# Two fused attention batches ahead of an MoE pair: V in rows of four tokens, pooled q and k summed by VectorE, and a replanned order

## The chip, the core and the metric

The kernel runs on one core of one Trainium2 chip. The metric is device time in microseconds (us), from the first to the last instruction of the program with what lies around them; lower is better. Engines: PE is TensorE (PEld its weight loads), DVE is VectorE, ACT is ScalarE, POOL is GpSimd, SP is SyncE, which here only issues DMAs.

## What is computed

Three steps in a row, with q, k, v of 4 batches x 8 heads x 576 tokens x 64:

```python
q_d = q.reshape(B, H, Sd, 4, D).mean(axis=3)          # the same for k_d, v_d; Sd = 144
out_up = np.repeat(sm_attn(q_d, k_d, v_d), 4, axis=2) # pooled attention, repeated
mask = np.abs(pos[:, None] - pos[None, :]) < 4        # banded attention, 7 keys a query
out = out_up + softmax(mask(scale * q @ k.T)) @ v
x = out.transpose(0, 2, 1, 3).reshape(2304, 512)
h = x @ w_in;  x = (h * sigmoid(h)) @ w_out           # 512 -> 2048 -> 512
h = x @ w2_in; g = s * relu(h) ** 2 + b
return g @ w2_out
```

The two weight pairs arrive as 64-bit floats and are turned into two 32-bit halves (high and low part) on the chip, by bit operations of DVE. Each product of the two layers is three matmuls of fp32r halves.

## The kernel before

The tokens are cut into five blocks (512, 512, 512, 512, 256). `mix1(u)` does the first layer of block u: for each of 16 slices m of the hidden dimension 12 matmuls into `hp`, SiLU, and 12 into `y0` to `y3`. The second layer follows for all blocks, into `hp2` and `o`. A 512-token block is 384 matmuls of 512 columns in each layer.

The attention of a batch is done for four pairs of heads (`hq` 0 to 3). Batches 2 and 3 take the banded part on DVE (`local`). Batches 0 and 1 take it on PE. For one pair:

- `tokens` loads q and k with a token on each partition (tiles `nq`, `nk`; the last 64 tokens of all heads come once, as `zq`, `zk`), `natural` loads v with eight tokens on each of 72 partitions (`nv`), `v_load` the band's copy of v (`vw`).
- `b_turn` turns q and k on PE (`pq`, L705 and L702) and ACT or DVE copy them to `qkT` (or `qT`, `kT`).
- `down` is the pooled attention. For batch 0 its sums of four tokens are PE matmuls with a 0/1 matrix `fours` (L596, L597, tile `pd`); for batch 1 they are DVE reductions of the turned tiles (L607, L609). v is summed by two DVE additions (L583, L584). Scores `pS` (L639), softmax, turns `pT` (L662), values `pU` (L671), kept in `upT`.
- `banded`: scores `pB` (L754), mask, softmax, turns `pBT` (L787), values `pBO` (L796), and the sum with `upT` into `xf` (L803).

`x_split` then cuts `xf` into `xh` (ACT, L535) and `xl` (DVE, L536), the two halves that the products of a block read. `weights(1, m)` loads `wi_raw` and `wo_raw` and splits each with L381, L384, L387, a cast (L314, ACT or DVE) and L391.

Nothing of this order is left to a hardware scheduler. `Weave` collects operations with an engine, a cost in us and a due number; `plan` simulates the engines with those costs and lists the operations in that order, and each engine's queue is filled in it. The planned start and end of each PE operation also decide fillers: where the plan shows PE idle for longer than `FILLG` in the first block's stage, that many tiny matmuls on zeros (`spin`, L354) are written into PE's queue:

```python
if begin[i] > FILL0 and 0 < left[self.idle] < 2 and begin[i] - now > FILLG:
    self.fill(int((begin[i] - now) * FILLD / 0.03))
```

100 more stand at the start. PE runs its queue in order, so a filler is run whether or not the next operation is ready. Operations marked `EITHER` go to ACT or DVE by the planned end and `BIAS`.

Of the kernel before, what the change touches and what calls it, by code (L numbers as in the profile page):

```python
# [36 lines left out]
BIAS = 0.6  # L37
START = 0.56
FLIGHT = 7
NW = 35  # L40
NACT, NACTV = 2, 1
# [8 lines left out]
NAT0, NATS = -3.092, 0.472  # L50
VW0, VWS, VW1 = -1.548, 0.219, -0.029
# [5 lines left out]
NAT1, PT1, PT1S = 0.05, 0.1, 0.2  # L57
# [205 lines left out]
def kernel(ctx, tc, q, k, v, w1_in, w1_out, w2_in, w2_out, s2, b2, cst, out):  # L263
# [30 lines left out]
    for tag, n in (("sc", 1), ("le", 1), ("mx", 1), ("sm", 1), ("rc", 1), ("bst", 3), ("dk", 1), ("de", 1), ("dst", 3)):  # L294
        kinds[tag] = slots(sp, tag, n)
# [38 lines left out]
    fours = fixed(cp, [P, P // 4], F32, "fours")  # L334
# [28 lines left out]
    def weights(layer, m, pr, after, lpr=None):  # L363
# [183 lines left out]
    def natural(b, i, names, kind, pr, after=[]):  # L547

        for nm in names:
            t = nat[b, i, nm] = Buf(kind, [QP, 2, 4, 2 * D], F32, "n" + nm)  # L550
            by = "act" if b == 0 and i < NACT else "sp"

            def load(t=t, nm=nm, by=by):
                for a in range(2):
                    dma(t[:].rearrange("p t r c -> p (t r) c")[:, :, a * D:(a + 1) * D], tens[nm][b, 2 * i + a].rearrange("(p e) d -> p e d", e=8),
                        nc.scalar if by == "act" else nc.sync)

            op(by, (2, 1.7, 0.82), load, w=[t], r=after, pr=pr)

    NT4 = S // P  # L560
    ends_of = {}

    def tokens(b, i, pr, kind, after=[]):

        for nm in "qk":
            if (b, nm) not in ends_of:
                ends_of[b, nm] = None
            t = nat[b, i, nm] = Buf(kind, [P, NT4, 2 * D], F32, "n" + nm)

            def load(t=t, nm=nm):  # L570
                for a in range(2):
                    row = (b * H + 2 * i + a) * S
                    dma(t[:, :, a * D:(a + 1) * D], bass.AP(tens[nm].tensor, row * D, [[D, P], [P * D, NT4], [1, D]]))

            op("sp", (2, 1.16, 0.73), load, w=[t], r=after, pr=pr)
            if ends_of[b, nm] is None:
                z = ends_of[b, nm] = Buf(kind, [S - NT4 * P, H, D], F32, "z" + nm)
                op("sp", (1, 0.6, 0.73), lambda z=z, nm=nm: dma(z[:], tens[nm][b, :, NT4 * P:, :].rearrange("h s d -> s h d")), w=[z], r=after, pr=pr)

# [7 lines left out]
    def down(b, i, pr, ps="ps"):  # L587
        qd, kd = q_diag[i % 2], Buf("dk", [P, SD], F32, "dk")
        if b == 0:
            sums = {"v": pool(b, i, "v", pr)}  # L590
            pt = Buf(ps, [P, 2, SD], F32, "pd")
            for j, nm in enumerate("qk"):
                def summed(j=j, nm=nm):
                    o = pt[:, j].rearrange("p (t n) -> p n t", t=2)
                    for c in range(NT4):
                        nc.tensor.matmul(o[:, c * 16:(c + 1) * 16], lhsT=nat[b, i, nm][:, c], rhs=fours.tile)  # L596
                    nc.tensor.matmul(o[:, NT4 * 16:], lhsT=ends_of[b, nm][:, 2 * i:2 * i + 2].rearrange("p a d -> p (a d)"), rhs=fours[:S - NT4 * P, :SD - NT4 * 32])  # L597

# [50 lines left out]
        op("pe", 0.73, score, w=[pS, (st, 1), e], r=[(qd, 0), (qd, 1), kd], pr=pr)  # L649
# [18 lines left out]
        for a in range(2):
            def value(a=a):
                for kt in range(2):  # L670
                    nc.tensor.matmul(pU[a * D:(a + 1) * D], lhsT=sums["v"](kt)[:, a * D:(a + 1) * D],  # L671
                                     rhs=at[:, kt, :, a * DQ:(a + 1) * DQ], start=(kt == 0), stop=(kt == 1))

            op("pe", 0.27, value, w=[(pU, a), (up, i)], r=[at, nat[b, i, "v"]], pr=pr)
# [12 lines left out]
    def b_turn(b, hq, pr, ps):  # L687
# [6 lines left out]
        for nm, (t, i) in (("q", bq[b, hq]), ("k", bk[b, hq])):  # L694
            for e in range(2):
# [14 lines left out]
                op("pe", 0.11 * n / P + 0.03, turn, w=[pt, (t, (i, e))], r=[r, csb], pr=pr)  # L710
                op(EITHER, (act(n), dve(n)), keep, w=[(t, (i, e))], r=[pt], pr=pr)

    def b_load(b, hqs, js, pr, after=[]):
# [22 lines left out]
        move = 0.2 * len(js) * len(hqs)  # L736
# [3 lines left out]
    def banded(b, hq, js, vw, vi, pr, ps, after=[]):  # L740
# [34 lines left out]
        op("pe", 0.13 * nb, score, w=[pB, e, (st, 0)], r=after + [(t, (i, e0)) for t, i in ((q_, qi), (k_, ki)) for e0 in range(2)], pr=pr)  # L775
# [13 lines left out]
        op("pe", 0.11 * nb, turn, w=[pT, at], r=[e, csb], pr=pr)  # L789
# [8 lines left out]
        op("pe", 0.11 * nb, value, w=[pO, key], r=[at, vw, (upT[b], hq)], pr=pr)  # L798
# [214 lines left out]
```

## Time and profile before

| | us |
|---|---|
| median of 3 runs | 942.54 (941.62 to 943.56) |
| the profiled execution | 944.93 |
| its span, first to last instruction | 943.0 |
| PE busy in the span | 924.8 |
| DVE, ACT busy in the span | 591.6, 418.1 |
| fillers (`spin`) on PE | 635 matmuls, the last at 78.1 |

The span is the time from the first to the last instruction of the profiled execution, whose own time is 1.9 us longer. PE's busy time counts every matmul until its modelled end, and fillers too, so that a busy PE is not a useful one.

### The profile page before, as it was taken

What the parts mean: (1) busy time and instruction counts of PE and PEld (TensorE: products, weight loads), DVE (VectorE), ACT (ScalarE), POOL (GpSimd) and SP (SyncE); (2) the same over time, 40 slices, a digit from 0 to 9 for tenths busy, and PEclk for the clock granted to TensorE, in tenths of its full rate; (3) what the DMA queues carried; (4) which work ended last, traced back from release to release, by engine and by line L of the source; (5) the groups of instructions that cost most, each with busy time, mean ns of one, the idle gap of its engine ahead of it and who ended that gap; (6) DMA issues with size and microseconds to landing.
All of it is one profiled execution on the core that took longest, in us unless ns stands there. A gap on an engine that the chain in (4) does not pass through costs nothing.

```text
span 943.0 us, 14244 instructions
## 1 busy us (share of the span) xinstructions
PE 924.8 (98%) x5575; PEld 765.5 (81%) x5575; DVE 591.6 (63%) x1120; ACT 418.1 (44%) x922; POOL 0.2 (0%) x4
## 2 busy tenths in 40 slices
PE   7999999999999999999999999999999999999997
PEld 7987677777787887778889988888888888888896
DVE  1789899768999999999229999232243224222332
ACT  2776787665646623343234544242233223222332
POOL 0000000000000000000000000000000000000000
PEclk7889999999999999999999999999999999999999
DMA  9988421263433412030029660020002000100000
GB/s 168 277 228 224 117 54 29 57 172 83 101 110 84 126 47 70 32 112 28 1 88 332 207 245 1 1 90 1 0 11 80 1 1 23 45 1 1 23 23 23
DMA packets 104509, 78.16 MB, mean 83 GB/s; under 512 B 70780, under 2 KB 90618, under 8 KB 104442
## 3 DMA queue, kind: packets, MB, share of 16 engines
q1 hardware_dynamic: 100902, 76.36, 28.2%
q10 hardware_dynamic: 3540, 0.89, 0.7%
q8 instruction: 44, 0.72, 0.3%
q14 instruction: 23, 0.19, 0.1%
HBM read 67.79 MB, written 9.44 MB: 82 GB/s over the span
## 4 chain that ended last, share of the span: by engine, by line
PE 83%; DVE 11%; DMA 3%; ACT 1%; issue 1%; SPq 0%; DVEq 0%; ACTq 0%
PE hp L813 36%; PE o L813 21%; PE y L813 15%; DVE tmp L497 2%; PE spin L354 2%; DMA nk<-in_k_dram 1%; PE pB L754 1%; PE pS L639 1%; DVE gl L834 1%; PE pBO L796 1%; PE pU L671 1%; DVE tmp L460 1%; DVE tmp L502 1%; DVE sc L463 1%; PE pBT L787 1%; DVE tmp L503 1%
## 5 line engine op out<-in xcount | busy, mean ns | idle before, releaser
L813 PE MATMUL hp<-xh,wi 128*128 128x512 f32 (+1 forms) x640 | 203.8, 379 | 2.0 <-ACT xh L535 1.2
L813 PE MATMUL y<-gh,wo 128*128 128x512 f32 (+1 forms) x640 | 201.3, 377 | 0.0
L813 PE MATMUL hp<-yh,wi 128*128 128x512 f32 (+1 forms) x640 | 186.1, 368 | 0.0
L813 PE MATMUL o<-wo,gh 128*128 128x512 f32 x576 | 177.5, 389 | 0.0
L942 DVE SCALAR_TENSOR_TENSOR gl<-r,sbt,gh 128x512 fp32r<-128x512 f32 (+1 forms) x80 | 55.8, 697 | 153.4 <-ACT gh L940 153.1
L813 PEld LDWEIGHTS hp<-xh,wi 128*128 128x128 f32 x640 | 116.8, 188 | 24.1 <-ACT g L832 1.9
L813 PEld LDWEIGHTS y<-gh,wo 128*128 128x128 f32 x640 | 117.0, 189 | 20.4 <-issue 0.8
L813 PEld LDWEIGHTS hp<-yh,wi 128*128 128x128 f32 x640 | 116.5, 188 | 20.2
L813 PEld LDWEIGHTS o<-wo,gh 128*128 128x128 f32 x576 | 107.7, 188 | 22.0
L940 ACT ACTIVATE gh<-r,sbt 128x512 fp32r<-128x512 f32 (+1 forms) x80 | 54.7, 684 | 157.5 <-PE o L813 149.8
L813 PE MATMUL y<-gl,wo 128*128 128x512 f32 (+1 forms) x320 | 118.3, 370 | 0.4 <-DVE gl L834 0.4
L813 PE MATMUL hp<-xl,wi 128*128 128x512 f32 (+1 forms) x320 | 118.2, 369 | 0.4 <-DVE xl L536 0.4
L813 PE MATMUL hp<-yl,wi 128*128 128x512 f32 (+1 forms) x320 | 117.7, 368 | 0.0
L813 PE MATMUL o<-wo,gl 128*128 128x512 f32 x288 | 112.0, 389 | 0.0
L938 DVE SCALAR_TENSOR_TENSOR r<-r,sbt 128x512 f32<-128x512 f32 (+1 forms) x80 | 55.8, 698 | 52.0 <-ACT r L937 51.8
L833 ACT CAST gh<-g 128x512 fp32r<-128x512 f32 (+1 forms) x80 | 46.3, 579 | 87.7 <-PE y L813 86.9
L834 DVE TENSOR_TENSOR gl<-g,gh 128x512 fp32r<-128x512 f32 (+1 forms) x80 | 50.5, 632 | 37.2 <-ACT gh L833 37.0
L937 ACT ACTIVATE r<-hp 128x512 f32<-128x512 f32 (+1 forms) x80 | 44.6, 557 | 64.9 <-DVE gl L942 46.5
L813 PEld LDWEIGHTS hp<-yl,wi 128*128 128x128 f32 x320 | 60.4, 189 | 10.2
L813 PEld LDWEIGHTS y<-gl,wo 128*128 128x128 f32 x320 | 60.5, 189 | 9.4 <-DVE gl L834 0.8
L813 PEld LDWEIGHTS hp<-xl,wi 128*128 128x128 f32 x320 | 60.5, 189 | 8.8 <-DVE xl L536 0.8
L832 ACT ACTIVATE g<-hp 128x512 f32<-128x512 f32 (+1 forms) x80 | 44.5, 557 | 42.9 <-DVE gl L834 36.2
(131 smaller groups left out, 1055.6 us busy)
## 6 DMA issues: line engine op xcount, KB each, us to landing
wi_raw<-in_moe_w_in_dram SPq DMA_DIRECT2D x32, 512.0 KB
wo_raw<-in_moe_w_out_dram SPq DMA_DIRECT2D x32, 512.0 KB
yd<-ys SPq DMA_DIRECT2D x16, 256.0 KB
yt<-yd SPq DMA_DIRECT2D x4, 1024.0 KB
nv<-in_v_dram SPq DMA_DIRECT2D x28, 144.0 KB
nq<-in_q_dram SPq DMA_DIRECT2D x16, 144.0 KB
nk<-in_k_dram SPq DMA_DIRECT2D x16, 144.0 KB
lk<-in_k_dram SPq DMA_DIRECT2D x6, 384.0 KB
```

The lines of the kernel that those rows point to most:

```text
L354: nc.tensor.matmul(spin[:], lhsT=idle[:], rhs=idle[:, :64], start=True, stop=True)
L460: op("dve", dve(n * WIN * D), lambda t=t, i0=i0, n=n, h2=h2: nc.vector.tensor_tensor(out=t[:], in0=wide(qs[:, h2, i0:i0 + n, :].unsqueeze( ...
L463: op("dve", dve(n * WIN * D), lambda t=t, i0=i0, n=n, h2=h2: nc.vector.tensor_reduce(out=sc[:, h2, i0:i0 + n, :], in_=t[:], axis=AX.X, op= ...
L497: op("dve", dve(n * WIN * D), lambda t=t, i0=i0, n=n, h2=h2: nc.vector.tensor_tensor(out=t[:], in0=wide(e[:, h2 * ns + i0:h2 * ns + i0 + n ...
L813: nc.tensor.matmul(t(), lhsT=lhs(i), rhs=rhs(i), start=(first and i == 0), stop=(last and i == 2))
L832: op("act", act(n), lambda g=g, hp=hp: nc.scalar.activation(out=g[:], in_=hp[:], func=AF.Silu), w=[g], r=[hp], pr=-5, table="silu")
L833: op("act", act(n), lambda g=g, gh=gh: nc.scalar.copy(out=gh[:], in_=g[:]), w=[gh], r=[g], pr=-5)
L834: op("dve", dve(n), lambda g=g, gh=gh, gl=gl: nc.vector.tensor_tensor(out=gl[:], in0=g[:], in1=gh[:].bitcast(F32), op=ALU.subtract), w=[gl ...
L937: op("act", act(n), lambda r=r, hp=hp: nc.scalar.activation(out=r[:], in_=hp[:], func=AF.Relu), w=[r], r=[hp], pr=-5)
L938: op("dve", dve(n) + 0.07, lambda r=r: nc.vector.scalar_tensor_tensor(out=r[:], in0=r[:], scalar=sbt[:, 0:1], in1=r[:], op0=ALU.mult, op1= ...
L940: op("act", act(n) + 0.1, lambda r=r, gh=gh: nc.scalar.activation(out=gh[:], in_=r[:], func=AF.Identity, bias=sbt[:, 1:2]), w=[gh], r=[r, ...
L942: op("dve", dve(n) + 0.07, lambda r=r, gh=gh, gl=gl: nc.vector.scalar_tensor_tensor(out=gl[:], in0=r[:], scalar=sbt[:, 1:2], in1=gh[:].bit ...
```

## The change

- V of batches 0 and 1 is loaded with four tokens on each of 128 partitions (1 KB pieces in place of 256 B), the last 64 tokens of all heads once as `zv`. Two DVE additions of 256 and 128 elements sum it; the 16 sums of `zv` come from one PE matmul (`pz`, 512 columns) a batch. The pooled keys are then cut as 128 and 16 in place of 72 and 72.
- Batch 0 sums its pooled q and k as batch 1 did, by DVE from the turned tiles, and the `fours` matmuls go.
- v of pairs 0 and 1 no longer goes through ACT's DMA queue (`NACT` 2 to 0).
- The plan's costs and due numbers are new, and with them the order on all queues, the fillers and some choices between ACT and DVE.

```diff
-BIAS = 0.6
+BIAS = 0.306
-FLIGHT = 7
+FLIGHT = 4
-NACT, NACTV = 2, 1
+NACT, NACTV = 0, 1
-NAT0, NATS = -3.092, 0.472
+NAT0, NATS = -2.916, 0.35
-RAWF, RAW0, RATE = -2.478, -1.951, 0.145
-DECF, DEC0, DECS = -2.194, -2.116, 0.268
-PT0, PTS = -3.336, 0.425
-PN0, PNS = -2, 0.052
+RAWF, RAW0, RATE = -2.478, -1.951, 0.212
+DECF, DEC0, DECS = -2.194, -2.054, 0.232
+PT0, PTS = -3.784, 0.425
+PN0, PNS = -2.779, 0.052
...
+def slow(ps):
+    return 1.25 if ps == "ps_first" else 1.1
...
+    def rows(b, i, names, pr, kind, after=[], by="sp"):
+        for nm in names:
+            t = nat[b, i, nm] = Buf(kind, [P, 2, NT4, D] if nm == "v" else [P, NT4, 2 * D], F32, "n" + nm)
...
+                if nm == "v":
+                    dma(t[:].rearrange("p a r d -> p a (r d)"), bass.AP(tens[nm].tensor, row * D, [[NT4 * D, P], [S * D, 2], [1, NT4 * D]]), queue)
+                    return
...
+    def pool_ends(b, pr, ps):
+        z = ends_of[b, "v"]
+        pz = Buf(ps, [NZ // 4, H * D], F32, "pz")
+        op("pe", 1.0, lambda: nc.tensor.matmul(pz[:], lhsT=four1[:NZ], rhs=z[:].rearrange("p h d -> p (h d)")), w=[pz], r=[z, four1], pr=pr)
+        op(EITHER, (act(H * D), dve(H * D)), lambda eng: copy(eng, z[:NZ // 4].rearrange("p h d -> p (h d)"), pz[:]), w=[z], r=[pz], pr=pr)
+
+    def pool_rows(b, i, pr):
+        t = nat[b, i, "v"]
+        op("dve", dve(4 * D), lambda: nc.vector.tensor_tensor(out=t[:, :, 0:2], in0=t[:, :, 0:2], in1=t[:, :, 2:4], op=ALU.add), w=[t], pr=pr)
+        op("dve", dve(2 * D), lambda: nc.vector.tensor_tensor(out=t[:, :, 0], in0=t[:, :, 0], in1=t[:, :, 1], op=ALU.add), w=[t], pr=pr)
...
     def down(b, i, pr, ps="ps"):
-        if b == 0:
-            sums = {"v": pool(b, i, "v", pr)}
-            pt = Buf(ps, [P, 2, SD], F32, "pd")
...
-                op("pe", 0.6, summed, w=[(pt, j)] + ([kd] if j else [(qd, 0), (qd, 1)]), r=[nat[b, i, nm], ends_of[b, nm], fours], pr=pr)
+        plain = (b, i) in bq
+        cuts = [(0, P), (P, SD)] if plain else [(0, QP), (QP, SD)]
+        if plain:
+            pool_rows(b, i, pr)
+            op("dve", dve(S), lambda: nc.vector.tensor_reduce(out=dq[:], in_=four(q_, qi), axis=AX.X, op=ALU.add), w=[dq], r=[(q_, (qi, e)) for e in range(2)], pr=pr)
+            op("dve", dve(S), lambda: nc.vector.tensor_reduce(out=kd[:], in_=four(k_, ki), axis=AX.X, op=ALU.add), w=[kd], r=[(k_, (ki, e)) for e in range(2)], pr=pr)
...
-        op("pe", 0.73, score, w=[pS, (st, 1), e], r=[(qd, 0), (qd, 1), kd], pr=pr)
+        op("pe", 0.9 * slow(ps), score, w=[pS, (st, 1), e], r=[(qd, 0), (qd, 1), kd], pr=pr)
...
-                op("pe", 0.11 * n / P + 0.03, turn, w=[pt, (t, (i, e))], r=[r, csb], pr=pr)
+                op("pe", (0.63 if e == 0 else 0.25) * slow(ps), turn, w=[pt, (t, (i, e))], r=[r, csb], pr=pr)
```

The other PE costs of `down` and `banded` are raised in the same manner. What the replanning does to PE's queue at the start, from pair 0's turn of q to its band scores (L705 is L716 after the change, L702 is L713, L754 is L765, L639 is L644, L354 is L357). Before:

```order
L705 MATMUL pq<-csb,nq 128x128 x4
L354 MATMUL spin<-idle 128x64
...
L702 MATMUL pq<-csb,zq 128x64 x4
L596 MATMUL pd<-fours,nq 128x16x2 x4
L597 MATMUL pd<-fours,zq 128x8x2
L705 MATMUL pq<-csb,nk 128x128 x4
...
L702 MATMUL pq<-csb,zk 128x64 x4
L596 MATMUL pd<-fours,nk 128x16x2 x4
L597 MATMUL pd<-fours,zk 128x8x2
L754 MATMUL pB<-qkT 64x72 x8
```

and after:

```order
L716 MATMUL pq<-csb,nq 128x128 x4
L713 MATMUL pq<-csb,zq 128x64 x4
L716 MATMUL pq<-csb,nk 128x128 x4
L713 MATMUL pq<-csb,zk 128x64 x4
L765 MATMUL pB<-qkT 64x72 x16
L589 MATMUL pz<-zv,four_80 16x512
L716 MATMUL pq<-csb,nq 128x128 x4
L644 MATMUL pS<-dk,q_diag_87 96x144 x3
```

The 46 fillers behind the first row, the 54 behind the turn of k, and all `pd` matmuls are gone, and `pz` is new. Over the whole program the fillers are 201 in place of 635: the 100 at the start, then 38, 32 and 31. The last 31 stand behind pair 3's `pBO`, where 85 stood.

DVE's queue at the end of the first block's attention, around the last `xl` (L803 and L536 are L814 and L539 after the change; the `f` tiles are weights being split; L381, L384, L387, L391 are L384, L387, L390, L394). Before:

```order
L391 TENSOR_TENSOR wi<-f_1309,wi 128x512
L381 TENSOR_SCALAR f_1417<-wi_raw 128x512
L803 TENSOR_TENSOR xf<-pBO,upT 128x256 x2
L391 TENSOR_TENSOR wo<-f_1327,wo 128x512
L384 SCALAR_TENSOR_TENSOR f_1417<-wi_raw,f_1417 128x512
L536 TENSOR_TENSOR xl<-xf,xh 128x512
```

and after:

```order
L394 TENSOR_TENSOR wi<-f_933,wi 128x512
L814 TENSOR_TENSOR xf<-pBO,upT 128x256 x2
L394 TENSOR_TENSOR wo<-f_933,wo 128x512
L384 TENSOR_SCALAR f_981<-wi_raw 128x512
L539 TENSOR_TENSOR xl<-xf,xh 128x512
```

Before, the weights split by then are slices m = 0 to 3 (f_1309 and f_1327 are slice 3); after, they are 0 to 2 (f_933 belongs to slice 2), so one slice's split comes behind the last `xl` that came ahead of it.

## Rows read from the trace of the kernel before

**Rows 1.** Busy time by stretch; columns as in the first line.
```profile
core 0: us, PE busy (x) PEld busy (x) DVE busy (x) ACT busy (x) POOL busy (x), PEclk, DMA share, GB/s
0.00:13.60 13.60, 8.65 (x164) 8.22 (x164) 3.21 (x8) 1.22 (x1) 0.20 (x4) 0.93 0.89 132
13.60:26.00 12.40, 12.38 (x120) 11.38 (x120) 2.23 (x6) 5.93 (x29) 0.00 (x0) 0.52 0.96 213
29.50:33.00 3.50, 3.50 (x48) 3.50 (x45) 1.92 (x5) 0.75 (x3) 0.00 (x0) 0.60 1.04 184
46.50:53.40 6.90, 6.90 (x93) 6.04 (x92) 4.16 (x12) 4.33 (x15) 0.00 (x0) 0.55 1.04 231
53.40:78.60 25.20, 24.45 (x457) 21.12 (x455) 22.34 (x59) 17.82 (x67) 0.00 (x0) 1.00 0.86 226
100.00:200.00 100.00, 100.00 (x708) 76.31 (x707) 84.72 (x210) 74.29 (x200) 0.00 (x0) 1.00 0.30 78
200.00:500.00 300.00, 295.26 (x1455) 236.86 (x1454) 243.36 (x420) 136.59 (x274) 0.00 (x0) 1.00 0.28 80
```

**Rows 2.** Chain that ended last, 5 to 79 us: start, us, what.
```profile
5.43 8.15 DMA nk<-in_k_dram
...
13.62 1.12 PE pq L705 x4
14.74 2.88 PE spin L354 x54
...
18.23 1.84 PE pd L596 x8
20.08 0.54 PE pd L597 x2
...
23.97 1.66 PE pS L639 x6
...
36.37 3.20 PE spin L354 x106
...
42.07 0.74 PE pS L639 x6
42.81 0.81 PE pd L596 x8
43.62 0.32 PE pd L597 x2
...
53.12 0.77 PE hp L813 x3
...
73.75 1.08 PE pBO L796 x32
74.83 1.53 PE spin L354 x49
```

**Rows 3.** Fillers alone, 13.6 to 74.8 us: PE busy, granted clock, DMA share, GB/s.
```profile
13.60:74.80 61.20, 16.43 (x405) 0.82 0.98 251
```

**Rows 4.** PE's waits, 13.7 to 78 us: us in total, times, longest.
```profile
PE spin L354 <- issue: 0.7, 1, 0.7
```

**Rows 5.** ACT's first wait, in the waits of 0 to 80 us.
```profile
ACT L316 <- DMA nv<-in_v_dram: 12.4, 1, 12.4
```

**Rows 6.** DVE operations by shape, 10 to 80 us: xcount | busy, mean ns | idle before.
```profile
L384 DVE SCALAR_TENSOR_TENSOR f<-wi_raw,f 128x512 int32<-128x512 int32 x5 | 3.4, 686 | 0.0
L381 DVE TENSOR_SCALAR f<-wi_raw 128x512 int32<-128x512 int32 x5 | 2.1, 414 | 0.0
L583 DVE TENSOR_TENSOR nv<-nv 72x512 f32<-72x512 f32 x3 | 2.0, 683 | 2.4 <-DMA nv<-in_v_dram 2.4
L584 DVE TENSOR_TENSOR nv<-nv 72x256 f32<-72x256 f32 x3 | 1.2, 407 | 0.0
```

**Rows 7.** Batch 1's pooled q, by tile: ns min/median/max, first and last start us.
```profile
L607 DVE TENSOR_REDUCE dq<-qkT x3: 741/743/755, 106.7 to 142.1; 128x144 f32<-128x576 f32 x3
```

**Rows 8.** DVE's instructions in order of time, 74 to 78 us.
```profile
74.48 0.82 DVE L803 TENSOR_TENSOR xf<-pBO,upT 128x256 f32<-128x256 f32 x2
76.42 0.68 DVE L536 TENSOR_TENSOR xl<-xf,xh 128x512 fp32r<-128x512 f32 x1
```

**Rows 9.** Busy time, 8 us to the end of the last xl.
```profile
8.00:77.10 69.10, 64.70 (x967) 57.89 (x963) 45.74 (x123) 42.38 (x161) 0.00 (x0) 0.83 0.98 237
```

More of the change, by code (lines that the diff above doesn't have):

```diff
@@ L333 @@
     band = fixed(cp, [P, BW], F32, "band")
-    fours = fixed(cp, [P, P // 4], F32, "fours")
+    four1 = fixed(cp, [P // 2, P // 8], F32, "four1")
     sbt = fixed(cp, [P, 2], F32, "sbt")
@@ L550, in natural @@
             t = nat[b, i, nm] = Buf(kind, [QP, 2, 4, 2 * D], F32, "n" + nm)
[L551 to L568, printed above, removed]
             def load(t=t, nm=nm):
                 for a in range(2):
[L572 to L578, printed above, removed]
+                    dma(t[:].rearrange("p t r c -> p (t r) c")[:, :, a * D:(a + 1) * D], tens[nm][b, 2 * i + a].rearrange("(p e) d -> p e d", e=8))
@@ new lines, in natural, with load @@
+            op("sp", (2, 2.3, 0.82), load, w=[t], r=after, pr=pr)
+    NT4 = S // P
+    NZ = S - NT4 * P
+    ends_of = {}
+    def rows(b, i, names, pr, kind, after=[], by="sp"):
+        for nm in names:
+            t = nat[b, i, nm] = Buf(kind, [P, 2, NT4, D] if nm == "v" else [P, NT4, 2 * D], F32, "n" + nm)
+            def load(t=t, nm=nm):
+                queue = nc.scalar if by == "act" else nc.sync
+                row = (b * H + 2 * i) * S
+                if nm == "v":
+                    dma(t[:].rearrange("p a r d -> p a (r d)"), bass.AP(tens[nm].tensor, row * D, [[NT4 * D, P], [S * D, 2], [1, NT4 * D]]), queue)
+                    return
+                for a in range(2):
+                    dma(t[:, :, a * D:(a + 1) * D], bass.AP(tens[nm].tensor, (row + a * S) * D, [[D, P], [P * D, NT4], [1, D]]), queue)
+            op(by, (1, 0.9, 0.5) if nm == "v" else (2, 1.55, 0.73), load, w=[t], r=after, pr=pr)
+            if (b, nm) not in ends_of:
+                z = ends_of[b, nm] = Buf(kind, [NZ, H, D], F32, "z" + nm)
+                op("sp", (1, 0.8, 0.73), lambda z=z, nm=nm: dma(z[:], tens[nm][b, :, NT4 * P:, :].rearrange("h s d -> s h d")), w=[z], r=after, pr=pr)
@@ L669, in value @@
             def value(a=a):
[L670 to L674, printed above, removed]
+                for kt, (k0, k1) in enumerate(cuts):
+                    if plain:
+                        rows = nat[b, i, "v"][:, a, 0] if kt == 0 else ends_of[b, "v"][:NZ // 4, 2 * i + a]
+                    else:
+                        rows = sums["v"](kt)[:, a * D:(a + 1) * D]
+                    nc.tensor.matmul(pU[a * D:(a + 1) * D], lhsT=rows, rhs=at[:k1 - k0, kt, :, a * DQ:(a + 1) * DQ], start=(kt == 0), stop=(kt == 1))
+            op("pe", 0.33 * slow(ps), value, w=[(pU, a), (up, i)], r=[at, nat[b, i, "v"]] + ([ends_of[b, "v"]] if plain else []), pr=pr)
         def keep(eng):
-            copy(eng, up[:, i, :].rearrange("p (n t) -> p t n", t=2), pU[:].rearrange("p (t n) -> p t n", t=2))
+            if plain:
+                copy(eng, up[:, i, :], pU[:])
+            else:
+                copy(eng, up[:, i, :].rearrange("p (n t) -> p t n", t=2), pU[:].rearrange("p (t n) -> p t n", t=2))
         op(EITHER, (act(SD), dve(SD)), keep, w=[(up, i)], r=[pU], pr=pr)
@@ L773, in norm @@
                     scale(eng, e[:, i], st[:, 2, i:i + 1])
-        op("pe", 0.13 * nb, score, w=[pB, e, (st, 0)], r=after + [(t, (i, e0)) for t, i in ((q_, qi), (k_, ki)) for e0 in range(2)], pr=pr)
+        op("pe", 0.155 * nb * slow(ps), score, w=[pB, e, (st, 0)], r=after + [(t, (i, e0)) for t, i in ((q_, qi), (k_, ki)) for e0 in range(2)], pr=pr)
         op("dve", dve(nb * KW, 2), mask, w=[e], r=[pB, band], pr=pr)
```

60 lines of the change are left out of this document (24 added, 36 removed).

## The prediction

> **What bounds the kernel now.** I read the busy time by stretch first [rows 1]. From 100 us on PE is busy all the time: 100.00 of 100 us, then 295.26 of 300. The work there is fixed by the products and hardly touched here, so what ends it earlier is an earlier start. The first block's attention stands before that, in 0 to 78.6 us, and there a busy PE says little, since fillers count. So the chain of waits comes next [rows 2]. From the landing of pair 0's k at 13.62 us to pair 3's last `pBO` at 73.75 us it stays on PE, but for an issue step or two: turns, `pd` sums, scores, and again and again `spin`. The list of PE's waits says the same from the other side: after 13.7 us it waited for no data and no other engine, only 0.7 us of issue [rows 4]. A queue that never waits while 405 fillers stand in it [rows 3] is a queue that fillers delay: the 54 behind the turn of k cost 2.88 us, the 106 at 36.37 us 3.20 us [rows 2]. DVE and ACT, which would be next, were busy 45.74 and 42.38 of the 69.10 us up to the last `xl` [rows 9]. So the stretch is PE-bound, and part of what binds it is not work.
>
> **The change part by part.** The sum goes from pair 0's k to the end of the first block's attention.
>
> Data. Pair 0's k landed at 13.6 us [rows 2]. Ahead of or beside it ran four v loads of 144 KB from ACT's queue (the first two pairs' v), which the change moves to SP behind pair 0's k. The stretch moved 132 GB/s [rows 1], so 576 KB less is 4.4 us, and k lands at about 9.2 us. On SP v of pair 0 and `zv` now stand ahead of the band mask, v of pair 1 ahead of the first weights, and pairs 2 and 3 ahead of the second weights. SP's queue gets longer by those issues, but the weights it delays are split late anyway. ACT no longer sits in its own DMA queue until 12.4 us [rows 5]; that wait hid behind the late k and is worth nothing alone.
>
> PE. Between 13.6 and 74.8 us the queue holds 61.2 us. Fillers are 404 of the chain's matmuls and take 15.3 us, summed over their pieces (first 2.88, 30 to 53 ns each [rows 2]; the view of the fillers gives 16.43 us with overlaps [rows 3]). `pd` takes 9.8 us: 1.84 + 0.54 for pair 0's k at the low clock, and seven sums at about 1.1, such as 0.81 + 0.32 [rows 2]. What remains is 36.1 us. The change puts back 38 and 32 fillers, 2.9 us at the mean of the two rates, and one `pz` of 512 columns. No such matmul was run. The nearest row is `pS`, 3 times 144 = 432 columns in 0.74 us at the full clock and in 1.66 at half [rows 2], which makes `pz` 0.9 to 2.0 us. I take 2.0, since it stands early, where the clock was low. Sum at the old clocks: 36.1 + 2.9 + 2.0 = 41.0 us in place of 61.2.
>
> Clock. The granted clock was 0.52 of full (mostly 1.2 GHz) in 13.6 to 26 us and 0.55 in 46.5 to 53.4, stretches in which PE was busy throughout, with fillers in only 2.9 and 1.4 us of them; from 53.4 on, with the first products in the queue, it was 1.00, which is 2.4 GHz [rows 1]. So I let everything up to the first product run at 1.2 GHz, and the rest at 2.4. Of the work before the first product, about 20 us, some 6.6 had run at the full clock in the old order (39.5 us up to 53.1, less 10.9 of fillers and 8.5 of `pd`, less 13.5 that lay in these two and in the low one of 29.5 to 33); they double. That makes 47.6 us.
>
> Waits. The old queue hid every wait for data or for a softmax under a filler. Taken out, the waits show. They are bounded by 0 and by the 15.3 us of fillers that covered them; I take 8.5, near the middle, because pair 2's q and k are read early (right behind pair 1's scores) while the trace shows the fillers of 14.74 and 36.37 us standing before operands that had been loaded long enough to be used at once. Then pair 3's last `pBO` ends at 9.2 + 47.6 + 8.5 = 65.3 us in place of 74.8, **9.5 us earlier**, and the last `xl` follows 2.3 us later as before, 77.1 less 74.8 [rows 2, 8].
>
> DVE. Batch 0 gets eight reductions of 576 elements, 743 ns each by batch 1's row [rows 7], 5.9 us. Its v sums fall from 512 and 256 elements (683 and 407 ns [rows 6]) to 256 and 128; with 407 for the first and, as no row has 128, 0.2 to 0.4 for the second, four pairs give back 1.6 us. Some 4 us more on 45.74 still fit into 8 to 67 us; with waits about as now DVE would be done near 66 us, just beside PE. So DVE is the next bound and the gain can't be much larger unless its waits shrink as well.
>
> Weights. One slice's split now comes behind the last `xl`. It is twice L381, two of the L384 kind and L391 of the same size, 2 x (0.41 + 3 x 0.686) = 4.9 us of DVE [rows 6]. Products of slice 3 start two slices after the first block's begin, so half of it should hide; I charge 2.5 us. Batch 1's `pz` lies on a full PE and costs 0.9 us at the full clock. The smaller v sums of batch 1 lighten DVE beside a busy PE; worth nothing. The replanned order in 200 to 500 us moves batches 2 and 3 between the products; PE was idle there for under 5 us [rows 1], so I give it nothing, plus or minus 3.
>
> Sum: -9.5 + 2.5 + 0.9 = **-6.1 us**. The profiled execution took 944.93 us, 2.4 above the median, so it would become 938.8, and the median 942.54 becomes 936.5. About 0.2%, 1.9 us, is what a measurement of this kernel can tell from no change.
>
> **The rivals.** First, *DVE and ACT follow the shorter queue*, and waits shrink to what pair 0 to 2's data need (0 to 3 us): `pBO` ends near 60 us, 14 earlier, and with half a microsecond for weights the time is 929. For it: both have over 23 idle us before the last `xl` [rows 9]. Against: then DVE would have to run 50 us of work without a gap from 9 us on.
>
> Second, *the split binds*: DVE was busy 22.34 of 25.20 us before the products and 84.72 of the next 100 [rows 1]. If batch 1's attention and the split can't be pulled forward together, PE waits for weights or for batch 1 in 70 to 190 us, and all but a microsecond or two goes: 941.5, no change that can be told.
>
> Third, on the other side, *the clock stays low*. The place is PE's queue from 9 to 75 us, the price the doubling of all that ran at 2.4 GHz. Of the 36.1 us of remaining work 22.6 had run there; at 1.2 GHz the queue is 36.1 + 22.6 + 2.0 + 3.7 (70 fillers at 53 ns) = 64.4 us, and with 3 us of waits the last `pBO` ends at 76.6, 1.8 later than now; with 2.5 for the weights and 0.9 for `pz` the time is about 947 to 948 as summed, 946 if the last of it warms. It decides from the point where the granted clock between 13 and 70 us falls under about 0.6; before, it was 0.82 in 13.6 to 74.8 [rows 3]. Against it: the products of block 0 begin before pair 3 is done, and with them the clock was full in the old order. The Trainium skill's page "TensorE: Matmul & The Clock Gate", section "Part 4: PE-mode transpose", says that transposes on PE don't count as activity for the clock as other matmuls do. A first stage that is mostly turns without fillers would by that rule stay at 1.2 GHz up to the products, which is this rival's condition up to there and my forecast's too; the low clock of the trace at 46.5 to 53.4 us, beside turns and band matmuls, agrees, and no row separates the turns from the rest.
>
> That the change does not do what it says I rule out for the fillers and `pd`, whose rows are gone from the queue; it could be so for the v loads, whose larger pieces may not move faster, but the sum takes nothing from that.
>
> **How the numbers follow.** The forecast 0.50 (between 932.5 and 940, by waits of 4.5 to 12 us), the shrinking waits 0.20, the split that binds 0.15, the low clock 0.15. Faster by over 0.2%, under 940.7: 0.50 + 0.20 + a third of the split's, 0.05, makes 0.75. Within 0.2%, up to 944.4: the rest of the split, 0.10, and a little of the low clock, 0.01. Slower: 0.14. The range leaves out a part of the first rival below 928.5 and most of the low clock above 944.5: 928.5 to 944.5.
>
> **What would show it.** Right: pair 0's k turned near 9 to 10 us; PE with real waits in 13 to 65 us; the last `xl` of block 0 near 67 to 68; the clock near half until the first product, then full; PE again without idle time from 100 us on. Wrong: a last `xl` at 75 or later with a granted clock under 0.6 (third rival); a last `xl` near 67 but PE waiting for `wi`, `wo` or batch 1's tiles afterwards (second); a last `xl` near 62 (first). A shift of more than 3 us that arises only after 200 us would mean that the replanned order of batches 2 and 3, which I set to nothing, decides.

## The result and the profile after

The changed kernel takes **929.31 us** (median of 4 runs, 928.93 to 929.74). The runs of the kernel before beside it have a median of 942.08, the ratio is 0.987 with a 95% interval of 0.984 to 0.991. The kernel before scatters: 65 executions beside all the runs below go from 934.54 to 945.82, median 940.5, and against that the change is worth 11.2 us (0.988, inside the interval). Forecast were 936.5 in a range of 928.5 to 944.5. The range holds the result, 0.8 us above its lower edge, but the gain is twice the forecast's, and it is the time of the first rival (929). The 0.2% that the forecast took as the least difference that can be told is less than half of this interval's width.

| | before, us | after, us |
|---|---|---|
| profiled execution, its span | 944.93, 943.0 | 928.93, 927.1 |
| PE, DVE, ACT busy in the span | 924.8, 591.6, 418.1 | 907.8, 594.9, 413.7 |
| pair 0's k turned at | 13.62 | 9.66 |
| its last 64 tokens (`zk`) turned at | 17.62 | 11.32 |
| last `pBO` of pair 3 ends | 74.83 | 55.16 |
| last `xl` of block 0 ends | 77.10 | 57.14 |

Busy time of the kernel after by stretch, beside [rows 1] and [rows 9] (first line: the columns):

```profile
core 0: us, PE busy (x) PEld busy (x) DVE busy (x) ACT busy (x) POOL busy (x), PEclk, DMA share, GB/s
9.00:57.20 48.20, 43.17 (x512) 31.89 (x513) 43.77 (x121) 36.54 (x149) 0.00 (x0) 0.90 1.05 276
9.66:55.16 45.50, 41.13 (x485) 30.30 (x485) 41.24 (x115) 35.73 (x147) 0.00 (x0) 0.90 1.05 273
0.00:13.60 13.60, 9.55 (x144) 8.57 (x146) 2.96 (x8) 4.24 (x13) 0.20 (x4) 0.82 1.00 154
13.60:20.00 6.40, 6.40 (x59) 4.50 (x56) 5.42 (x15) 3.55 (x18) 0.00 (x0) 0.57 1.05 279
20.00:26.00 6.00, 5.24 (x74) 4.31 (x70) 5.85 (x20) 5.96 (x25) 0.00 (x0) 1.00 0.95 217
26.00:57.20 31.20, 28.14 (x357) 20.20 (x357) 30.70 (x85) 25.17 (x100) 0.00 (x0) 1.00 1.06 300
57.20:80.00 22.80, 21.14 (x110) 15.24 (x107) 22.66 (x50) 17.91 (x33) 0.00 (x0) 1.00 0.95 260
100.00:200.00 100.00, 99.75 (x722) 74.61 (x722) 79.29 (x207) 75.26 (x205) 0.00 (x0) 1.00 0.33 89
200.00:500.00 300.00, 296.65 (x1467) 239.93 (x1462) 246.14 (x418) 127.97 (x253) 0.00 (x0) 1.00 0.30 90
```

From 26 us to the last `xl` DVE is busy 30.70 of 31.20 us and PE 28.14: the first stage has changed its bound. From 100 us on PE is as full as before. The chain that ended last says the same; where [rows 2] stayed on PE, from 19 us on it now goes mostly over DVE and ACT:

```profile
4.59 6.69 DMA zk<-in_k_dram
11.32 0.69 PE pq L713 x4
12.01 2.11 PE pB L765 x32
14.12 1.81 PE pz L589 x2
...
28.04 0.64 DVE dq L614
...
31.34 0.64 DVE dq L614
...
36.54 0.65 DVE dk L615
...
42.20 1.47 ACT be L777 x8
...
54.05 1.11 PE pBO L807 x32
55.52 0.68 DVE wo L394
56.54 0.60 DVE xl L539
57.14 0.60 DVE f L387
...
59.35 1.28 ACT L843
60.65 0.61 ACT g L843
61.30 0.74 PE hp L824 x2
```

Behind the last `xl` it stays on DVE (`f`, a weight split) and then on ACT, whose table load (1.28 us, L843) and SiLU the next `hp` waits for. PE's waits from pair 0's k to the last `pBO`, beside [rows 4] (us in total, times, longest):

```profile
PE pT L667 <- DVE de L328: 1.2, 1, 1.2
PE pq L716 <- DMA nk<-in_k_dram: 1.0, 1, 1.0
PE pU L680 <- ACT dat L318: 1.0, 2, 0.8
PE pBT L798 <- ACT be L326: 0.6, 1, 0.6
```

There are waits now, but short ones. The end of the stage in DVE's queue, beside [rows 8]:

```profile
54.72 0.89 DVE L814 TENSOR_TENSOR xf<-pBO,upT 128x256 f32<-128x256 f32 x2
55.52 0.68 DVE L394 TENSOR_TENSOR wo<-f,wo 128x512 fp32r<-128x512 f32 x1
56.46 0.68 DVE L539 TENSOR_TENSOR xl<-xf,xh 128x512 fp32r<-128x512 f32 x1
```

The last `xl` ends at 57.14, **20.0 us earlier**. Counted in the trace, 129 products have run by 90 us where it was 56. They follow each other 0.227 us apart, so 73 of them are 16.5 us. At 200 us the lead is 45 products and at 450 us 67 (15.2 us), so it moves with what else stands between the products, and the spans differ by 15.9. So all of the gain comes from the first 57 us, and about 4 us of it are given back behind them; these counts don't show where. The two profiled executions lie further apart than the medians (16.0 against 12.8 us), because the one before took 944.93 us.

The comparisons leave out four of the ten executions of one kernel below (`a_pd`, 951 to 953 us, its profiled one among them), in which its clock fell lowest; its ratio rests on the other six, whose median is 942.85.

### The profile page after: what moved, and what is told of

It is laid out like the page before. It is cut to its first block, busy times and chain, and to the rows that moved or that the text cites. A ratio compares the mean times of both kernels' runs of the same rounds, so it can differ in the third digit from the quotient of the medians.

```text
span 927.1 us, 13217 instructions
## 1 busy us (share of the span) xinstructions
PE 907.8 (98%) x5065; PEld 738.9 (80%) x5065; DVE 594.9 (64%) x1137; ACT 413.7 (45%) x911; POOL 0.2 (0%) x4
## 4 chain that ended last, share of the span: by engine, by line
PE 75%; DVE 16%; ACT 4%; DMA 2%; issue 1%; SPq 0%; ACTq 0%; DVEq 0%
PE hp L824 34%; PE o L824 21%; PE y L824 14%; DVE tmp L500 3%; DVE tmp L463 2%; DVE sc L466 2%; DVE tmp L505 2%; DVE gl L845 2%; DVE tmp L506 1%; PE pU L680 1%; PE pS L644 1%; PE pB L765 1%; PE pBO L807 1%; DVE pv L507 1%; DMA zk<-in_k_dram 1%
## 5 line engine op out<-in xcount | busy, mean ns | idle before, releaser
L843 ACT ACTIVATE g<-hp 128x512 f32<-128x512 f32 (+1 forms) x80 | 44.4, 556 | 48.1 <-DVE gl L845 45.2
```

The lines of the kernel that those rows point to most:

```text
L843: op("act", act(n), lambda g=g, hp=hp: nc.scalar.activation(out=g[:], in_=hp[:], func=AF.Silu), w=[g], r=[hp], pr=-5, table="silu")
```

## The experiments

The names are those of the runs: `a_` is the changed kernel with an edit, `b_` the kernel before.

| run | median us (runs) | ratio to before, 95% | clock | last `xl` ends | split by then | fillers |
|---|---|---|---|---|---|---|
| b_nofill | 945.48 (10) | 1.0043 (1.0025, 1.0060) | 0.983 | 72.2 | 4, 4 | 101 |
| a_refill | 934.07 (4) | 0.9929 (0.9904, 0.9954) | 1.000 | 60.7 | 3, 3 | 609 |
| a_nofill | 931.89 (4) | 0.9901 (0.9882, 0.9921) | 0.985 | 60.4 | 3, 3 | 101 |
| a_pd | 947.39 (10) | 1.0024 (0.9991, 1.0056) | 0.971 | 81.0 | 5, 5 | 200 |
| a_pd_even4 | 944.95 (10) | 1.0051 (1.0026, 1.0075) | 0.994 | 74.0 | 5, 5 | 405 |
| a_v8act | 932.68 (4) | 0.9901 (0.9879, 0.9922) | 0.997 | 65.0 | 4, 3 | 506 |
| b_newplan | 942.73 (10) | 1.0014 (0.9992, 1.0037) | 0.991 | 68.6 | 5, 4 | 336 |
| a_oldconst | 937.91 (7) | 0.9966 (0.9940, 0.9992) | 0.992 | 63.0 | 5, 5 | 443 |
| a_oldpe | 940.28 (10) | 1.0007 (0.9982, 1.0031) | 0.991 | 57.3 | 2, 2 | 549 |
| a_oldpe_late | 932.17 (5) | 0.9920 (0.9894, 0.9946) | 0.989 | 57.6 | 3, 3 | 201 |
| a_dve2 | 936.10 (4) | 0.9942 (0.9921, 0.9962) | 0.988 | 63.1 | 3, 3 | 201 |
| a_warm | 930.32 (6) | 0.9876 (0.9855, 0.9896) | 0.997 | 57.8 | 3, 3 | 273 |

The clock is the mean granted one of the profiled execution, whose last `xl` stands beside it. "Split by then" counts the slices of `wi` and of `wo` that DVE had split when that `xl` ended: 4 and 4 in the kernel before (635 fillers), 3 and 3 in the kernel after (201). The plan sets this number, and a slice is 4.9 us of DVE, so where it differs the last `xl` does not stand for the same work.

**The fillers.** My main argument was that fillers delayed PE's queue.

```diff
-FILL0, FILLG, FILLD = 5.0, 0.477, 0.95
+FILL0, FILLG, FILLD = 1e9, 0.477, 0.95
```

on the kernel before:

> The kernel before with no fillers behind the 100 at the start; order of all real work as before. Theory 'fillers' (they delayed the first stage in PE's in-order queue): of the 61.2 us between pair 0's k and pair 3's last pBO the 15.3 us of fillers go and some waits show, so the last xl of block 0 comes at 65 to 69 us in place of 77.1 and the time is 932 to 937 us. Rival 'order and rows' (the new order, V rows and pooled sums gave the gain, fillers only filled time that was idle): last xl at 75 to 77, time 940 to 943. Rival 'clock' (fillers hold the clock up): granted clock under 0.6 from 14 to 53 us, last xl at 77 or later, time 943 or more.

Busy time of this run by stretch (columns as above), and then PE's waits in it (us in total, times, longest):

```profile
13.60:72.20 58.60, 50.81 (x498) 42.73 (x498) 43.33 (x119) 40.64 (x160) 0.00 (x0) 0.81 0.94 246
...
30.00:35.00 5.00, 1.47 (x10) 1.05 (x10) 4.85 (x19) 4.99 (x26) 0.00 (x0) 1.00 0.88 243
35.00:50.00 15.00, 15.00 (x120) 13.30 (x120) 8.43 (x23) 8.15 (x28) 0.00 (x0) 0.54 1.04 270
50.00:72.20 22.20, 18.15 (x231) 14.18 (x228) 21.24 (x59) 17.09 (x66) 0.00 (x0) 1.00 0.81 234
```

```profile
PE pq L705 <- DMA nk<-in_k_dram: 4.9, 2, 4.1
PE pT L662 <- DVE de L324: 2.6, 1, 2.6
PE pBT L787 <- DVE be L770: 1.8, 1, 1.8
```

The last `xl` came 4.9 us earlier in this execution, about half of what the theory wanted. It is the fastest of the ten, with 940.39 us; the others have mean clocks of 0.973 to 0.979 and no trace, and the median is 0.4% slower than before. Two things ate the gain. Half of the 15.3 us of fillers had covered waits that were there anyway: PE now idles 7.8 of 58.6 us. And after PE had idled (1.47 us busy in 30 to 35 us) the clock stood at 0.54 for 15 us, in which PE was busy throughout and DVE and ACT only half. The first theory falls as the main cause; the clock rival holds in time alone, for in this execution the mean clock of 14 to 53 us was 0.72, not under 0.6, and the last `xl` was early.

```diff
+REFILL = 6
...
+                if begin[i] > FILL0 and 0 < left[self.idle] < 2:
+                    self.fill(REFILL)
                 now = finish[i]
```

on the kernel after:

> The changed kernel with 6 fillers ahead of every PE operation of the first stage, about 400 more; order of all real work as after. Theory 'fillers': 400 at 38 ns (15.3 us / 404 in the kernel before) are 15 us of queue, of which 5 us fall into PE's idle time between 9 and 57 us, so the last xl comes near 67 us in place of 57.1 and the time is 936 to 941. Rival 'order and rows': last xl at 57 to 60, time 929 to 931. Rival 'DVE binds the stage so that PE's queue hardly matters': last xl at 59 to 62, time 930 to 934.

Busy time from 9 us to this run's last `xl`:

```profile
9.00:60.70 51.70, 51.59 (x874) 42.27 (x872) 43.90 (x121) 37.99 (x150) 0.00 (x0) 1.00 1.08 281
```

408 fillers make PE full again (51.59 of 51.70 us) and cost 3.6 us at the last `xl` and 4.8 in all. They also hold the clock at 1.00, which the kernel after has at 0.90 up to there. So fillers cost, but this is 4.8 of 11 us, and both numbers fit the rival in which PE's queue hardly matters (the time to 0.1 us).

Without the fillers that are left behind the start (first edit, on the kernel after; 100 of the 101 go, the last one stays):

> The changed kernel without the 101 fillers that are left behind the 100 at the start; order as after. Theory 'DVE binds now' (43.8 of 48.2 us busy from 9 us to the last xl): the 3.0 us of fillers lay in PE time that nothing waited for, last xl at 56 to 57.5, time 928 to 930. Theory 'PE still binds': last xl 2 to 3 us earlier, 926 to 927. Rival 'clock': granted clock from 13.6 to 40 us falls below 0.75 where it was 0.78 and 1.00, last xl at 60 or later, time 932 to 938.

```profile
9.00:60.40 51.40, 46.94 (x423) 32.89 (x423) 43.92 (x121) 37.60 (x153) 0.00 (x0) 0.77 1.12 284
13.60:20.00 6.40, 5.70 (x26) 3.46 (x23) 5.21 (x15) 3.47 (x18) 0.00 (x0) 0.50 1.16 302
20.00:26.00 6.00, 5.98 (x56) 4.84 (x57) 5.39 (x17) 5.88 (x24) 0.00 (x0) 0.63 1.20 233
```

The busy time by stretch bears the clock rival out, at the edge of its range: 0.63 where it was 1.00, 0.50 again in 55 to 60 us, the last `xl` 3.2 us later and 2.6 us more; over 13.6 to 40 us the mean was 0.79, though, not below 0.75. The fillers, of which the 70 before the last `pBO` take 2.4 us, earn more than they cost. And DVE does not bind alone: up to the last `xl` it did the same work as in the kernel after (43.92 against 43.77 us) and idled 7.5 us in place of 4.4.

**The parts of the change, one undone at a time.** The pooled q and k of batch 0 back on PE:

```diff
+            if b == 0:
+                pt = Buf(ps, [P, 2, SD], F32, "pd")
...
+                        for c in range(NT4):
+                            nc.tensor.matmul(pt[:, j, c * 32:(c + 1) * 32], lhsT=nat[b, i, nm][:, c], rhs=four1.tile)
...
+                op("pe", 1.2, summed, w=[(pt, j)] + ([kd] if j else [(qd, 0), (qd, 1)]), r=[nat[b, i, nm], ends_of[b, nm], four1], pr=pr)
```

> The changed kernel with one part undone: the pooled q and k of batch 0 are again summed by PE (eight sums with the 0/1 matrix) in place of eight DVE reductions; V rows, costs and due numbers as after. Theory 'the work moved off PE' (PE was full in the first stage, and eight sums of about 1.13 us are 9 us): PE's 43.2 busy us between 9 and 57 us less 3.0 of fillers plus 9.0 are 49.2 and some waits, last xl at 60 to 65 us in place of 57.1, time 931 to 936. Rival 'DVE binds there': DVE loses 5.9 us of reductions, last xl at 53 to 57, time 926 to 929. Rival 'the order alone': last xl at 56 to 59, time 929 to 931.

It costs more than any theory expected: by the ratios (1.0024 against 0.987) 1.5% over the kernel after, all of the gain. Its executions go from 936.77 us at a mean clock of 0.991 to 953.46 at 0.971, and the clock gives their order almost alone. The same with fillers spread evenly:

```diff
+EVEN = 4
-FILL0, FILLG, FILLD = 5.0, 0.477, 0.95
+FILL0, FILLG, FILLD = 5.0, 1e9, 0.95
...
+                if begin[i] > FILL0 and 0 < left[self.idle] < 2:
+                    self.fill(EVEN)
```

> The changed kernel with batch 0's pooled q and k summed by PE again (as in the run of that part alone) and the planned fillers replaced by 4 ahead of each PE operation of the first stage, 305 behind the 100 in place of 100. Theory 'clock' (that run lost 18 us because its clock stood at 0.50 over most of 9 to 71 us, while DVE was idle; its fastest execution, at a mean clock of 0.991, took 936.8): granted clock 1.00 throughout, little scatter, time 931 to 936 although 205 fillers are added. Rival 'the sums' own PE time': last xl at 70 or later at a clock of 1.00, time 938 to 945.

Busy time of this run in two stretches:

```profile
9.00:20.00 11.00, 11.00 (x99) 9.65 (x98) 2.60 (x7) 3.60 (x16) 0.00 (x0) 0.55 1.00 235
20.00:74.00 54.00, 53.05 (x702) 42.44 (x699) 47.27 (x124) 37.18 (x139) 0.00 (x0) 1.00 0.91 248
```

The rival holds. At a clock of 1.00 from 20 to 74 us PE is full (53.05 of 54.00) and the last `xl` comes at 74.0. With the sums on PE the stage is PE-bound, and here fillers that hold the clock cost about as much as they save (944.95 us against the 942.85 of `a_pd`). With the sums on DVE neither weighed as much: 408 more fillers cost 4.8 us, the clock without fillers 2.6. These two runs have five slices split ahead of the last `xl`; `a_oldconst` below has as many, with the sums on DVE, other due numbers and 443 fillers, and its last `xl` comes 11 us earlier, at 63.0.

V with eight tokens a partition again, the first two pairs on ACT's queue:

```diff
-NACT, NACTV = 0, 1
+NACT, NACTV = 2, 1
...
-        cuts = [(0, P), (P, SD)] if plain else [(0, QP), (QP, SD)]
+        cuts = [(0, QP), (QP, SD)]
...
-            pool_rows(b, i, pr)
+            sums = {"v": pool(b, i, "v", pr)}
```

> The changed kernel with another part undone: V of batches 0 and 1 with eight tokens on each of 72 partitions again, the first two pairs' loads on ACT's DMA queue, no pz; pooled sums by DVE, costs and due numbers as after. Theory 'data' (pair 0's k landed 4 us earlier because of this): k turned near 13.5 us in place of 9.7, last xl 3 to 5 us later (60 to 62), time 931 to 934. Rival 'DVE and ACT work ahead meanwhile': k late but last xl at 57 to 59, time 929 to 931.

PE's wait for k, and the stage:

```profile
PE pq L713 <- DMA nk<-in_k_dram: 4.2, 1, 4.2
```

```profile
13.60:65.10 51.50, 43.98 (x742) 37.03 (x742) 47.39 (x126) 37.85 (x149) 0.00 (x0) 0.97 1.02 271
```

As 'data' expected in time (3.4 us more), later in the stage (last `xl` at 65.0, not 62): k is late again, and DVE, which has the longer V sums again and a fourth slice of `wi` ahead of the last `xl`, is busy 47.39 of the 51.50 us to it. That V's rows and queue set when k lands is shown, and that DVE and ACT do not hide it. What the early k is worth alone is not: the plan of this run also writes 305 more fillers than that of the kernel after, 54 of them right behind the turn of k.

**The plan.** The new due numbers, `BIAS`, `FLIGHT` and PE costs on the code before:

```diff
-BIAS = 0.6
+BIAS = 0.306
-FLIGHT = 7
+FLIGHT = 4
...
-        op("pe", 0.73, score, w=[pS, (st, 1), e], r=[(qd, 0), (qd, 1), kd], pr=pr)
+        op("pe", 0.9 * slow(ps), score, w=[pS, (st, 1), e], r=[(qd, 0), (qd, 1), kd], pr=pr)
```

> The kernel before (V eight tokens a partition, pooled sums of batch 0 on PE, V on ACT's queue) planned with the changed kernel's due numbers, BIAS, FLIGHT and PE costs; 336 fillers in place of 635. Theory 'work moved off PE and early data': k still lands near 13.5 us and the 10 us of sums stay, last xl at 66 to 72, time 935 to 940. Rival 'order': the order carries most of it, last xl at 58 to 64, time 929 to 934. Rival 'clock': fewer fillers, granted clock under 0.6 over 13 to 50 us, last xl at 72 or later, 940 or more.

The last `xl` falls in 'work moved off PE' (68.6, in the fastest of the ten executions), the time above it: 942.7 is no gain. The plan alone is worth nothing on the old code. The reverse, old due numbers, `BIAS` and `FLIGHT` on the new code:

> The changed kernel's code and PE costs planned with the old due numbers, BIAS 0.6 and FLIGHT 7; 443 fillers. Theory 'work moved off PE and early data': last xl at 57 to 63 us, time 930 to 935. Rival 'order': old due numbers give the gain back, last xl at 65 or later or PE waiting for batch 1's tiles in 100 to 200 us, time 937 to 942.

Between the two: the last `xl` is the first theory's (63.0, with five slices split by then), the time the rival's (937.9, 8.6 us more than after), though PE waits for nothing of batch 1 in 100 to 200 us. The old PE costs on the new code:

```diff
-        op("pe", 0.9 * slow(ps), score, w=[pS, (st, 1), e], r=[(qd, 0), (qd, 1), kd], pr=pr)
+        op("pe", 0.73, score, w=[pS, (st, 1), e], r=[(qd, 0), (qd, 1), kd], pr=pr)
...
-                op("pe", (0.63 if e == 0 else 0.25) * slow(ps), turn, w=[pt, (t, (i, e))], r=[r, csb], pr=pr)
+                op("pe", 0.11 * n / P + 0.03, turn, w=[pt, (t, (i, e))], r=[r, csb], pr=pr)
```

> The changed kernel planned with the old, smaller PE costs of the attention (one part undone: the measured durations); code, due numbers and other costs as after. The plan then sees PE idle more often and writes 549 fillers in place of 201, and the order moves a little. Theory 'fillers': like the kernel with 400 put back, last xl at 65 to 70, time 936 to 941. Rival 'order and rows' (due numbers, V rows and DVE's sums carry the gain): last xl at 57 to 60, time 929 to 932.

Neither theory: the time is the first one's (940.3), the last `xl` the rival's (57.3), with 549 fillers. Here is the stage, then 130 to 200 us, and PE's largest waits in the latter:

```profile
9.00:57.30 48.30, 46.50 (x841) 38.04 (x838) 41.56 (x118) 36.69 (x144) 0.00 (x0) 1.00 1.02 268
130.00:200.00 70.00, 64.71 (x431) 48.27 (x431) 53.46 (x128) 42.26 (x111) 0.00 (x0) 0.95 0.27 69
```

```profile
PE hp L824 <- ACT g L843: 1.6, 2, 1.3
PE y L824 <- ACT gh L844: 1.2, 1, 1.2
PE pB L765 <- ACT de L648: 0.9, 1, 0.9
```

The loss comes behind the stage. PE idles 5.3 of 70 us, mostly for ACT (0.25 us in the kernel after), and the clock falls to 0.95. The costs change the order in which ACT and DVE serve batch 1 and the products. And the equal last `xl` hides work put off: only two slices are split by then where it was three. To see whose costs these are, the old ones only behind the first stage:

```diff
+        op("pe", 0.9 * slow(ps) if ps == "ps_first" else 0.73, score, ...
```

> The changed kernel with the old, smaller PE costs only for the attention behind the first stage (batch 1 and the rest of batch 0's band); the first stage, its order and its 201 fillers as after. Theory 'planned costs of batch 1' (with old costs everywhere the last xl came at 57.3 us as after, and 12 us were lost between 100 and 500 us, PE idle for 5.3 us and the clock at 0.94 to 0.96 in 130 to 200): last xl at 57, PE waits in 130 to 200 us, time 934 to 940. Rival 'the first stage's order decides' (its fillers and what stands between them shift what DVE and ACT reach by 100 us): time 929 to 931.

932.2, between the theories: the first stage is as after, and 2.9 us are lost, not in 130 to 200 us but later (busy time by stretch):

```profile
300.00:540.00 240.00, 233.27 (x1231) 196.66 (x1230) 192.50 (x342) 96.04 (x182) 0.00 (x0) 0.99 0.34 109
```

PE idles 6.7 us there, where it idles 2.2 in the kernel after. By difference some 8 of the 11 us hang on the first stage's costs, although its last `xl` is at the same time in both. How they do so is not settled: the old costs put a slice's split, 4.9 us of DVE, behind the last `xl` and change what of batch 1 DVE and ACT have done by 100 us, but no run separates these.

**The new bound.** Each of the eight reductions twice:

```diff
+            twice = lambda o, x: [nc.vector.tensor_reduce(out=o[:], in_=four(*x), axis=AX.X, op=ALU.add) for _ in range(1 + (b == 0))]
+            op("dve", dve(S), lambda: twice(dq, (q_, qi)), w=[dq], r=[(q_, (qi, e)) for e in range(2)], pr=pr)
+            op("dve", dve(S), lambda: twice(kd, (k_, ki)), w=[kd], r=[(k_, (ki, e)) for e in range(2)], pr=pr)
```

> The changed kernel with each of batch 0's eight pooled sums on DVE done twice (8 more reductions of 743 ns, 5.9 us on DVE); planned costs and order as after. Theory 'DVE binds the first stage' (43.8 of 48.2 us busy): last xl at 61 to 63.5 us in place of 57.1, time 932.5 to 935.5. Rival 'PE's chain binds and DVE has 4.4 us of slack': last xl at 57 to 59, time 929 to 931.

Busy time from 9 us to the last `xl`, and that `xl` in DVE's instructions in order of time:

```profile
9.00:63.20 54.20, 47.45 (x513) 35.17 (x513) 49.67 (x129) 37.46 (x148) 0.00 (x0) 0.81 1.01 272
```

```profile
62.44 0.69 DVE L539 TENSOR_TENSOR xl<-xf,xh 128x512 fp32r<-128x512 f32 x1
```

5.9 us more of DVE move the last `xl` by 6.0 us, to 63.13, and the time by 6.8, 0.6 us above the theory's range. The clock fell too, to 0.81 in the stage, and the run without fillers shows that this can move the last `xl` by itself. But there DVE idled 7.5 us, and here 4.5, as in the kernel after (4.4): the work was added one to one, and DVE binds.

**A better version?** 72 more fillers where PE waits for the first q and k:

```diff
+EVEN = 6
...
+                if begin[i] > FILL0 and 0 < left[self.idle] < 2 and nth <= 12:
+                    self.fill(EVEN)
+                nth += 1
```

> The changed kernel with 72 more fillers, 6 ahead of each of the first 12 PE operations (up to pair 0's band scores), where PE waited 3.1 us for q and k; the rest as after. Theory 'clock' (pair 0's turns and band scores ran at 0.50 from 9 to 14 us because PE had idled): granted clock 1.00 from 9 to 20 us, pair 0's work 1.5 to 2.5 us earlier, last xl at 55 to 56, time 927 to 928.5. Rival 'DVE binds from 14 us on': clock 1.00 there and last xl within 0.7 us of 57.1, time 928.8 to 930. Against: fillers delay the turns, 930 to 931.

Busy time of the start:

```profile
9.00:13.60 4.60, 3.70 (x52) 2.87 (x51) 1.47 (x4) 2.41 (x9) 0.00 (x0) 0.89 0.84 179
13.60:20.00 6.40, 6.40 (x94) 5.19 (x92) 4.58 (x12) 3.47 (x18) 0.00 (x0) 0.81 1.03 278
```

The clock rises from 0.50 and 0.57 to 0.89 and 0.81, and nothing is won: 930.3 us, last `xl` at 57.8. That fits DVE as the bound. No run beats the kernel after.

## Why the prediction was right in sign and short by half

- **Data: right.** k was put at about 9.2 us and is turned at 9.66, its last 64 tokens (`zk`), which the forecast left out, at 11.32; the wait for them is 0.6 us. With V undone k waits 4.2 us again. The 3.4 us of that run are not the price of this alone.
- **PE's work: right.** The queue without clock and waits was put at 41.0 us: 36.1 of work, 2.9 of fillers, 2.0 of `pz`. It is 41.13 busy us, with 2.4 of fillers and 1.9 of `pz` (1.81 in the chain). That it fits so closely is in part luck: the 41.0 were taken at the old clock, a mean of 0.82, and the mean is now 0.90. The 9.8 us of `pd` are right, but they are pair 0's k and six sums of 1.13 to 1.33 us, not seven.
- **Clock: the term that failed first.** I added 6.6 us, letting all up to the first product run at 1.2 GHz. The clock was at half only to about 19 us and then at 1.00, some 20 us before the products begin:

```profile
L824 PE MATMUL hp<-xl,wi x320: 280/389/402, 40.4 to 522.0; 128*128 128x512 f32 x128, 128*128 128x256 f32 x32
```

  (the tile's own view: ns min/median/max, first and last start in us.) My own rows said so: the mean was 0.82 over 13.6 to 74.8 us [rows 3], and I had counted 6.6 us of work at the full clock before the first product. I took two low stretches for the rule. The Trainium skill's "TensorE: Matmul & The Clock Gate", section "Part 4: PE-mode transpose", by which transposes do not count as PE-busy the same way, had leaned me that way. The row of 20 to 26 us shows a full clock on turns, scores and band matmuls without products, which is not what the forecast made of that rule; no run separates the turns. 38 fillers stand from 19.06 to 20.33 us and no more until 45.5, and without them (`a_nofill`) the clock rose only at 24.4 us. But in the kernel after it rose at 19.05, as the first of them began, so that they raised it is not shown.
- **Waits: mis-sized.** Taken were 8.5 us, the middle of 0 to 15.3; there are 4.4 (45.50 less 41.13). With 0.5 for the later k this closes the sum: 65.3 - 6.5 - 4.1 + 0.5 = 55.2. A middle of bounds was the wrong choice: the floor was to be had from DVE. The forecast put DVE's work at about 50 us without taking off the slice's split, 4.9 us by its own row, that moves behind the last `xl`; measured are 43.77 from 9 us to that `xl`.
- **DVE as the next bound: right, and shown** by the doubled reductions. It was ready not "near 66 us" but at 57. So the first rival came true, nearly with its own condition: from 26 us to the last `xl` DVE idles 0.5 us. That its time, 929, is hit to 0.3 us is luck in part: it put the last `pBO` near 60 us, which is 55.16, and half a microsecond behind it, where some 4 are lost. The other two rivals did not come true: from the last `xl` to 200 us PE waits for no weights and for no tile of batch 1, and the clock of the stage was 0.90.
- **Weights and `pz` of batch 1: right in size, the place not shown.** Charged were 3.4 us; of the 20.0 some 4.1 are missing at the end. To be seen are batch 1's `pz`, 1.03 us at 75.57, and one wait of `hp` for SiLU, 1.7 us where it was 0.8. **The order of 200 to 500 us: right**, nothing, but only with the new costs: with the old ones behind the stage 2.9 us go, and PE idles in 300 to 540.
- **The reason given: only partly right.** "A queue that fillers delay" is what I put first, and taking the fillers away from the kernel before gives nothing. What the earlier end of the stage rests on is the work moved off PE, which ends PE's hold on the stage and most of its exposure to the clock; whether that reaches the time hangs on the plan as well. No part was shown to do it alone, and no run moves only the sums in the kernel before. The undone parts cost 3.4 (V, with more fillers), 8.6 (due numbers), 11.0 (PE costs) and, by the ratios, 14 us (sums), far more than the 11 to 13 together. That fits one bound that is of no use released while another holds, but how the costs and due numbers bind stays open.

## What to carry to other kernels

A PE that never waits, with fillers in its queue, is not yet a PE delayed by them: ask how much of the fillers covers waits, and what clock they hold. Take the floor of a stage from the next engine's busy time, less what the plan moves out of the stage, not from a share of the covered waits. In a planned kernel an edit and its plan belong together: undo parts singly, expect losses that do not add up, and look at what else each new plan changes: fillers, and the work put ahead of the mark that is compared.

## What was not expected of the hardware

The scatter of the kernel before goes with its clock. Of 65 executions the 13 at a mean granted clock under 0.9875 have a median of 942.8 us, the 10 above 0.9935 one of 937.9; a straight line through all gives 0.64 us for each 0.001. In the one execution with a trace the clock that is missing stands in the first stage (0.83 over 8 to 77 us [rows 9], 1.00 from 100 us to 500). A busy PE did not bring it back there: in the kernel before without fillers it stayed at 0.54 for 15 us with PE busy 15.00 of 15.00. Nor did a busy PE always keep it up: in the kernel before it fell to half at 45.9 us, with PE busy 3.90 of 3.90 us ahead of that. What lets it rise in one stretch and fall in another stays open.
